# Attention and two MLPs on one core: due times of weight conversions and of transposed copies

## The chip, the cores and the metric

One core of a Trainium2 chip runs the whole program. The metric is the device time of one execution in microseconds; below 0.5% two kernels cannot be told apart.

## The reference

Attention over 2 batches and 12 heads of 448 positions and 64 dimensions, with scores capped by tanh, and then two MLPs of 768 to 2048 to 768 on the 896 tokens that come out:

```python
scores = cap * np.tanh(np.matmul(q, k.transpose(0, 1, 3, 2)) / np.sqrt(64) / cap)
attn = np.exp(scores - np.max(scores, axis=-1, keepdims=True))
attn = attn / (np.sum(attn, axis=-1, keepdims=True) + 1e-09)
x = np.matmul(attn, v)                      # then heads side by side: 896 x 768
h = x @ w_in;  g = np.where(h > 0, h, np.exp(np.minimum(h, 0)) - 1);  x = g @ w_out
h = x @ w_in2; out = np.maximum(0.01 * h, h) @ w_out2
```

The inputs are float32 but for the weights, which come as 64-bit floats (two 32-bit words each).

## The kernel before

**Attention.** Two heads of one batch make a pair; there are twelve, numbered 0 to 11. For a pair TensorE transposes k and q (L343, tiles `ntk`, `ntq`, which share one PSUM bank), VectorE copies them out (L358 `kT`; L354 `qT`, with a scale), TensorE makes the scores in four pieces (L371, `sc10.0` to `sc10.3` for pair 10; two banks of PSUM take turns), ScalarE takes tanh and exp (L391, L399, tiles `e10.0`, `e10.1` of two pieces each), POOL adds the two pieces of each (L408, `s10.0`, `s10.1`) and VectorE adds the halves (L414). TensorE multiplies with v (L496, `po`) and sums the rows (L510, `sm`); VectorE takes the reciprocal (L516, `rec`) and multiplies (L524, `xf`). ScalarE rounds that to the short format (L303, `xh`) and VectorE takes the remainder (L306, `xl`): each product of the MLPs is three products of rounded parts and remainders. The steps of neighbouring pairs are interleaved: the reciprocal of pair n falls between the scores of pairs n+1 and n+2, and the transposes for pair n+1 beside those of pair n.

**Weights.** `w_in` comes in slabs (`g1.0` to `g1.15` for the first MLP), `w_out` in slabs `o1.00.0` and so on. For each, SyncE loads the raw words (L549, `raw...`, three buffers), ScalarE scales the upper word (L555, `wg1.0`), VectorE shifts the lower word right (L562; for later slabs ScalarE does this, L567) and merges it and the sign in (L576, L585). `split` then rounds (ScalarE, L303, `g1.0h`) and takes the remainder (VectorE, L306, `g1.0l`). So one early slab of w_in costs VectorE four steps. The MLP's first product (L646) needs `g1.0h` and `g1.0l`.

**The order.** Nothing is in the order of the code. `plan(engine, cost, fn, ...)` records a step; `Plan.order()` runs all of them against a table of costs, engine by engine, and always takes the step that can start first and, among those, the one with the smallest `late` (the latest start that keeps its due time and those of its followers). The engines then execute their lists in that order, and a step that waits holds up all behind it on its engine. A step with `calm` (conversions due before `TM`, and `xh` and `xl`) may not be placed more than `AHEAD` before its `late` (L125). POOL's adds, `xl`, the adds of halves and the VectorE steps of conversions are marked `port`: the planner never lets two of them overlap. `TP = 9.0` is the planner's time for a pair, `TM = 12.6 * TP` its end of attention; the three first slabs are due 24 us before it and later (L878).

Of the kernel before, what the change touches and what calls it, by code (L numbers as in the profile page):

```python
# [23 lines left out]
class Plan:  # L24
# [8 lines left out]

    LATENCY = dict(PE=0.27, ACT=0.12, DVE=0.1, POOL=0.1, SP=0.1)
    LANDING = 2.0
    AHEAD = 12.0
    STAY = 2.0
    SWITCH = 0.12

# [33 lines left out]
    def order(self):  # L73
# [39 lines left out]
        def earliest(o):  # L113
# [10 lines left out]
            if o["calm"]:  # L124
                t = max(t, o["late"] - self.AHEAD)  # L125
            if o["gp"]:
# [67 lines left out]
def attention_elu_mlp_leaky_mlp(  # L194
# [55 lines left out]
    with tc.If((bits & 0x7FFFFFFF) <= CAP_BOUND_BITS, preferred_fallthrough_block=True) as small:  # L250
        block(*args, bounded=True)
    with small.Else():
        block(*args, bounded=False)
# [3 lines left out]
def block(ctx, tc, consts, q, k, v, w_in1, w_out1, w_in2, w_out2, out, bounded):  # L257
# [37 lines left out]
    plan = Plan(CAPACITY)  # L295
    V = {}

    def tl(pool, tag, name, shape, dtype=F32):
        V[name] = pools[pool].tile(shape, dtype, tag=tag, name=name, bufs=CAPACITY[tag])
        return V[name]  # L300
# [33 lines left out]
    def transpose_nat(nm, n, at):  # L334

        name, pt = f"{nm}T{n}", f"nt{nm}{n}"

        tag = "sm" if n == 0 and nm == "q" else "nt"

        def fn():  # L340
            t = tl("ps", tag, pt, [P, 512])
            for c in range(NC):
                nc.tensor.matmul(  # L343
                    t[:, c * CP : (c + 1) * CP], V[f"n{nm}{n}"][:, c], ident[:CP, :CP],
                    is_transpose=True, start=True, stop=True,
                )

        plan("PE", 0.39, fn, reads=[f"n{nm}{n}"], writes=[pt], new={pt: tag}, at=at, att=True,
             kind="transpose")

        def evacuate():
            t = tl("att", nm + "T", name, [P, S])
            if nm == "q":
                nc.vector.tensor_scalar(  # L354
                    out=t, in0=V[pt][:, :S], scalar1=qscale, scalar2=None, op0=ALU.mult
                )
            else:
                nc.vector.tensor_copy(t, V[pt][:, :S])  # L358

        plan("DVE", 0.6, evacuate, reads=[pt], writes=[name], new={name: nm + "T"}, att=True)  # L360

    def scores(n, c, at):

# [228 lines left out]
    def split(name, to, due=None):  # L592
        hi, lo = to + "h", to + "l"
        calm = CALM if due is not None and due < TM else 0.0
        plan("ACT", 0.73, lambda: rounded(tl("w", "whi", hi, V[name].shape, F32R), V[name]),
             reads=[name], writes=[hi], new={hi: "whi"}, due=due, calm=calm)
        plan("DVE", 0.87, lambda: remainder(tl("w", "wlo", lo, V[name].shape, F32R), V[hi], V[name]),
             reads=[name, hi], writes=[lo], new={lo: "wlo"}, port=True, due=due, calm=calm)

    def in_src(w, m):  # L600
        return w[:, m * P : (m + 1) * P, :].rearrange("(k p) f t -> p k f t", p=P)

    def out_src(w, k2, half):
        src = w[2 * k2 * P : (2 * k2 + 2) * P, half * HALF : (half + 1) * HALF, :]
        return src.rearrange("(k p) e t -> p k e t", p=P)
# [243 lines left out]
    for n in range(NPAIR):  # L849
        T = (n + 0.3) * TP  # L850
        load("k", k, n)
        load("q", q, n)
        load("v", v, n)
        transpose_nat("k", n, T - 0.95 * TP)
        transpose_nat("q", n, T - 0.8 * TP)
        if n == 0:

            plan("PE", 0.4, lambda: nc.tensor.matmul(
                tl("ps", "po", "unused", [P, 512])[:, :P], busy, busy, start=True, stop=True),
                writes=["unused"], new={"unused": "po"}, at=T - 0.7 * TP, att=True)  # L860
        for c in range(NC):
            scores(n, c, T + c * TP / 4)
        (bounded_softmax if bounded else row_softmax)(n)
        for c in range(NC):
            attend(n, c, T + (c + 3.6) * TP / 4)
        if bounded:
            sums(n, T + 7.4 * TP / 4)
        x1(n, T + 2.6 * TP)
    TH = 6 * KM * MM
    TO = 3 * MS * (KF // 2) * MM  # L870
    T0 = TM
    for nm, w_in, w_out in (("1", w_in1, w_out1), ("2", w_in2, w_out2)):
        slabs = [(i, h, k2) for i, h in ((0, 0), (1, 0), (1, 1), (0, 1)) for k2 in range(K2)]
        for m in range(KF):
            due = T0 + m * TH - 12.0
            if nm == "1" and m < 3:

                due = min(due, T0 - 24.0 + 2.5 * m)  # L878
            convert(f"g{nm}.{m}", in_src(w_in, m), f"wg{nm}.{m}", "wa", due)
            split(f"wg{nm}.{m}", f"g{nm}.{m}", due + 2.0)  # L880
            hidden(nm, m, T0 + m * TH)
        for x, (i, h, k2) in enumerate(slabs):
            due = T0 + (x + 1) * TH if nm == "2" else TM + x * KF * TH / len(slabs)
            convert(f"o{nm}.{i}{h}.{k2}", out_src(w_out, h * K2 + k2, i), f"w{nm}.{i}{h}.{k2}", "w", due)
        products(nm, T0 + KF * TH)
        T0 += KF * TH + 7 * TO
# [44 lines left out]
```

## Time and profile before

| | us |
|---|---|
| median of 3 runs | 575.94 (574.22 to 576.28) |
| profiled execution, own time | 572.52 |
| its span | 570.7 |
| TensorE busy | 554.6 (97%) |
| VectorE busy | 482.8 (85%) |
| ScalarE busy | 386.6 (68%) |
| POOL busy | 53.9 (9%) |
| mean granted TensorE clock | 0.994 |
| loads of k, q, v: issue to landing, median | 3.3, 3.4, 2.7 |

Busy time is the union of an engine's instructions; the granted clock is a share of full speed. Times in the rows are counted from the start of the span. The attention takes the first 115 us, the first MLP runs to about 335 us, the second to the end.

### The profile page before, as it was taken

The page shows a single profiled execution, that of the slowest core. Times are in us where ns is not written, and L with a number is a line of the kernel's source. Part 1 is how long each engine was busy: PE and PEld are TensorE (multiplying, and loading weights), DVE is VectorE, ACT ScalarE, POOL GpSimd, SP SyncE. Part 2 cuts the span into 40 slices and gives each one's busy share as a digit, 9 for nine tenths or more (in the row PEclk, how much of TensorE's full clock was granted, in tenths as well). Part 3 has the DMA queues.
Part 4 walks back from the last instruction along what each step waited for, and adds up shares of the span by engine and source line. Part 5 has one row for each costly group of instructions (what it writes and reads, how often), then busy time and mean ns, then how long its engine had stood idle before and what let it go on. Part 6 is the DMA issues. An engine that isn't in the chain of part 4 may idle for free.

```text
span 570.7 us, 7409 instructions
## 1 busy us (share of the span) xinstructions
PE 554.6 (97%) x2750; PEld 452.7 (79%) x2750; DVE 482.8 (85%) x628; ACT 386.6 (68%) x539; POOL 53.9 (9%) x32
## 2 busy tenths in 40 slices
PE   8999998899999999999999999999999999999995
PEld 4333333279999999899989999999999999889994
DVE  2698899896888998999999978888997599997662
ACT  5888997946888888865566766766775255645550
POOL 2544544410000000000000000000000000000000
PEclk9999998999999999999999999999999999999998
DMA  8933324215767777500012117766672000001112
GB/s 157 249 68 96 82 65 128 71 57 172 224 206 203 198 215 219 168 2 1 1 55 56 56 57 222 208 199 206 208 202 83 0 2 1 1 1 48 49 35 68
DMA packets 61435, 61.89 MB, mean 108 GB/s; under 512 B 23248, under 2 KB 53200, under 8 KB 61392
## 3 DMA queue, kind: packets, MB, share of 16 engines
q1 hardware_dynamic: 61120, 61.23, 38.2%
q8 instruction: 23, 0.38, 0.3%
q14 instruction: 20, 0.16, 0.1%
q10 hardware_dynamic: 240, 0.11, 0.1%
q0 software_dynamic: 32, 0.00, 0.0%
HBM read 58.59 MB, written 2.75 MB: 107 GB/s over the span
## 4 chain that ended last, share of the span: by engine, by line
PE 80%; DVE 10%; ACT 6%; issue 2%; POOL 1%; DMA 1%; SPq 0%; DVEq 0%; ACTq 0%; POOLq 0%
PE acc L646 27%; PE acc L751 23%; PE acs L751 11%; PE po L496 2%; DVE rec L516 2%; PE sm L510 1%; PE ct L807 1%; DMA firstq<-in_q_dram 1%; PE acs29.1_3302 L646 1%; PE acs6.0_1238 L646 1%; PE acs35.0_3687 L646 1%; PE acs32.0_3491 L646 1%; PE acs26.1_3112 L646 1%; PE acs12.1_1635 L646 1%; PE acs3.1_1022 L646 1%
## 5 line engine op out<-in xcount | busy, mean ns | idle before, releaser
L516 DVE RECIPROCAL rec<-sm 128x448 f32<-128x448 f32 x12 | 35.4, 2954 | 3.1 <-PE sm L510 3.0
L358 DVE COPY kT<-ntk 128x448 f32<-128x448 f32 x12 | 7.5, 622 | 7.4 <-PE ntk L343 7.0
L822 ACT COPY ob<-ct 112x512 f32<-112x512 f32 (+1 forms) x8 | 4.5, 560 | 10.5 <-PE ct L807 10.2
L343 PEld LDWEIGHTS ntq<-ident,nq 112*128 112x128 f32 x44 | 4.3, 140 | 8.8 <-DVE kT L358 8.1
L354 DVE TENSOR_SCALAR qT<-ntq,qscale 128x448 f32<-128x448 f32 x12 | 8.2, 681 | 3.5 <-PE ntq L343 3.5
L343 PEld LDWEIGHTS ntk<-ident,nk 112*128 112x128 f32 x44 | 4.3, 140 | 7.8 <-issue 7.1
L524 DVE TENSOR_TENSOR xf<-po,rec 128x448 f32<-128x448 f32 x12 | 7.5, 625 | 0.4
L343 PE MATMUL ntq<-ident,nq 112*128 112x112 f32 x44 | 6.6, 273 | 0.8 <-DVE kT L358 0.8
L343 PE MATMUL ntk<-ident,nk 112*128 112x112 f32 x44 | 6.6, 273 | 0.0
L567 ACT ACTIVATE rawo1.00.2_978<-rawo1.00.2_978,third 128x768 int32<-128x768 uint8 x1 | 1.0, 1028 | 7.8 <-DMA rawo1.00.2_978<-in_moe_w_out_dram 7.8
L371 PE MATMUL sc10.0_795<-qT,kT 64*112 64x448 f32 x4 | 1.8, 1010 | 2.6 <-DVE qT L354 2.6
L675 ACT ACTIVATE ea2.14.0_3955<-acs38.0_3883 128x448 f32<-128x448 f32 x1 | 0.5, 546 | 5.4 <-PE acs38.0_3883 L646 5.4
L820 DVE COPY ob<-ct 112x512 f32<-112x512 f32 (+1 forms) x5 | 3.2, 637 | 1.1 <-ACT ob L822 0.6
L666 DVE SCALAR_TENSOR_TENSOR gg1.0.0_1080<-ea1.0.0_1068,acc 128x448 f32<-128x448 f32 x1 | 0.6, 620 | 4.1 <-ACT ea1.0.0_1068 L663 4.1
L660 ACT ACTIVATE ea1.0.0_1068<-acc 128x448 f32<-128x448 f32 x1 | 0.5, 547 | 5.1 <-DMA rawo1.00.3_1049<-in_moe_w_out_dram 5.1
L238 PE MATMUL unused<-busy 128*128 128x128 f32 x12 | 2.9, 434 | 1.1 <-DVE third L244 1.1
L303 ACT CAST th2.7.3_4004<-gg2.3.1_3278 128x448 fp32r<-128x448 f32 x1 | 0.6, 569 | 5.0 <-PE acs L751 5.0
L391 ACT ACTIVATE e0.0_155<-sc0.0_147 112x896 f32<-112x896 f32 x1 | 0.9, 917 | 4.0 <-PE sc0.0_147 L371 4.0
L238 PEld LDWEIGHTS unused<-busy 128*128 128x128 f32 x12 | 2.6, 330 | 1.1 <-DVE third L244 1.1
L788 DVE TENSOR_TENSOR c2.00.0_4963<-u2.1.0_4292,acc 128x448 f32<-128x448 f32 x1 | 0.6, 621 | 3.2 <-PE acc L751 3.2
L263 DVE TENSOR_SCALAR ncap<-capb 128x1 f32<-128x1 f32 x1 | 0.2, 154 | 3.7 <-DMA capb<-in_cap_dram 3.7
L408 POOL TENSOR_TENSOR s9.0_787<-e9.0_733 112x896 f32<-112x896 f32 x1 | 3.0, 3050 | 2.2 <-ACT e9.0_733 L399 2.2
(4974 smaller groups left out, 2266.9 us busy)
## 6 DMA issues: line engine op xcount, KB each, us to landing
nv<-in_v_dram SPq DMA_DIRECT2D x12, 224.0 KB, 2.7
nk<-in_k_dram SPq DMA_DIRECT2D x11, 224.0 KB, 3.3
nq<-in_q_dram SPq DMA_DIRECT2D x11, 224.0 KB, 3.4
out_dram<-ob SPq DMA_DIRECT2D x3, 672.0 KB, 4.3
rawg1.0_203<-in_moe_w_in_dram SPq DMA_DIRECT2D x1, 768.0 KB, 7.3
rawg1.1_248<-in_moe_w_in_dram SPq DMA_DIRECT2D x1, 768.0 KB, 6.1
rawg1.2_282<-in_moe_w_in_dram SPq DMA_DIRECT2D x1, 768.0 KB, 7.5
rawo1.00.0_764<-in_moe_w_out_dram SPq DMA_DIRECT2D x1, 768.0 KB, 4.9
```

The lines of the kernel that those rows point to most:

```text
L238: nc.tensor.matmul(t, busy, busy, start=True, stop=True)
L343: nc.tensor.matmul(t[:, c * CP : (c + 1) * CP], V[f"n{nm}{n}"][:, c], ident[:CP, :CP], is_transpose=True, start=True, stop=True,)
L354: nc.vector.tensor_scalar(out=t, in0=V[pt][:, :S], scalar1=qscale, scalar2=None, op0=ALU.mult)
L358: nc.vector.tensor_copy(t, V[pt][:, :S])
L496: nc.tensor.matmul(V[po][j * D : (j + 1) * D, :S], V[f"nv{n}"][:, j, c], V[e][:, c % 2, j], start=(c == 0), stop=(c == NC - 1),)
L510: nc.tensor.matmul(t[j * D : (j + 1) * D, :S], ones[:CP], V[f"s{n}.0"][:, j], start=True, stop=True,)
L516: plan("DVE", 2.97, lambda: nc.vector.reciprocal(out=tl("att", "rec", rec, [P, S]), in_=V[sm][:, :S]), reads=[sm], writes=[rec], new={rec: ...
L524: nc.vector.tensor_tensor(out=tl("att", "xf", xf, [P, S]), in0=V[po][:, :S], in1=V[f"rec{n}"], op=ALU.mult)
L646: nc.tensor.matmul(bank(where[b]), V[g + w][:, kt, :], V[f"{part}{nm}.{b}.{kt}"], start=(x == 0 and i == 0), stop=(x == KM - 1 and i == 2),)
L751: nc.tensor.matmul(bank(where[m]), V[sp][:, kt % 2, m * P : (m + 1) * P], V[tp], start=(kt == 0 and i == 0), stop=(kt == KF // 2 - 1 and i ...
L807: nc.tensor.matmul(t[:CP, x * P : (x + 1) * P], V[c][:, x * CP : (x + 1) * CP], ident, is_transpose=True, start=True, stop=True,)
L822: nc.scalar.copy(dst, src)
```

## The change

Three numbers. The planner may place a calm step 60 us ahead of its latest start instead of 12. The copies `kT` and `qT` get a due time 2 us behind the planned time of their transposes (before, they inherited theirs from the scores that read them). The first three slabs of w_in are due 18 us before the end of attention instead of 24.

```diff
     LANDING = 2.0
-    AHEAD = 12.0
+    AHEAD = 60.0
     STAY = 2.0
@@ transpose_nat
-        plan("DVE", 0.6, evacuate, reads=[pt], writes=[name], new={name: nm + "T"}, att=True)
+        plan("DVE", 0.6, evacuate, reads=[pt], writes=[name], new={name: nm + "T"}, att=True, due=at + 2.0)
@@ the loop over slabs
             if nm == "1" and m < 3:
-                due = min(due, T0 - 24.0 + 2.5 * m)
+                due = min(due, T0 - 18.0 + 2.5 * m)
```

What that does to the lists is seen at three places. On VectorE (DVE), between the copy of k and the copy of q for pair 10, the list of before reads:

```order
L358 COPY kT_745<-ntk_737 128x448
L576 SCALAR_TENSOR_TENSOR wg1.0_700<-wg1.0_700,rawg1.0_203 128x768
L585 SCALAR_TENSOR_TENSOR wg1.0_700<-rawg1.0_203,wg1.0_700 128x768
L414 TENSOR_TENSOR s8.0_696<-s8.0_696,s8.1_728 112x896
L562 TENSOR_SCALAR rawg1.1_248<-rawg1.1_248 128x768
L576 SCALAR_TENSOR_TENSOR wg1.1_726<-wg1.1_726,rawg1.1_248 128x768
L306 TENSOR_TENSOR xl1.1.3_781<-xf_735,xh1.1.3_761 128x448
L585 SCALAR_TENSOR_TENSOR wg1.1_726<-rawg1.1_248,wg1.1_726 128x768
L354 TENSOR_SCALAR qT_789<-ntq_749,qscale 128x448
L516 RECIPROCAL rec_793<-sm_773 128x448
```

and now, at the same copies:

```order
L358 COPY kT_765<-ntk_757 128x448
L414 TENSOR_TENSOR s8.0_716<-s8.0_716,s8.1_748 112x896
L354 TENSOR_SCALAR qT_777<-ntq_769,qscale 128x448
L562 TENSOR_SCALAR rawg1.2_282<-rawg1.2_282 128x768
L306 TENSOR_TENSOR xl1.1.3_801<-xf_755,xh1.1.3_779 128x448
L516 RECIPROCAL rec_803<-sm_792 128x448
L524 TENSOR_TENSOR xf_825<-po_735,rec_803 128x448
L414 TENSOR_TENSOR s9.0_787<-s9.0_787,s9.1_808 112x896
L358 COPY kT_834<-ntk_820 128x448
```

The conversions of slabs 0 and 1 have left this place. They stand some four pairs earlier. There, on VectorE, from the reciprocal of pair 4 to that of pair 5, the list of before has none:

```order
L516 RECIPROCAL rec_521<-sm_510 128x448
L524 TENSOR_TENSOR xf_535<-po_452,rec_521 128x448
L414 TENSOR_TENSOR s5.0_503<-s5.0_503,s5.1_525 112x896
L358 COPY kT_549<-ntk_537 128x448
L354 TENSOR_SCALAR qT_563<-ntq_553,qscale 128x448
L306 TENSOR_TENSOR xl1.0.2_580<-xf_535,xh1.0.2_565 128x448
L516 RECIPROCAL rec_586<-sm_576 128x448
```

and now:

```order
L585 SCALAR_TENSOR_TENSOR wg1.0_396<-rawg1.0_203,wg1.0_396 128x768
L516 RECIPROCAL rec_526<-sm_519 128x448
L524 TENSOR_TENSOR xf_544<-po_458,rec_526 128x448
L306 TENSOR_TENSOR xl1.1.1_552<-xf_476,xh1.1.1_504 128x448
L358 COPY kT_558<-ntk_546 128x448
L414 TENSOR_TENSOR s5.0_512<-s5.0_512,s5.1_532 112x896
L562 TENSOR_SCALAR rawg1.1_248<-rawg1.1_248 128x768
L354 TENSOR_SCALAR qT_577<-ntq_564,qscale 128x448
L306 TENSOR_TENSOR xl1.0.2_593<-xf_544,xh1.0.2_575 128x448
L576 SCALAR_TENSOR_TENSOR wg1.1_403<-wg1.1_403,rawg1.1_248 128x768
L516 RECIPROCAL rec_602<-sm_589 128x448
```

A merge of slab 0, a shift and a merge of slab 1 have come in, the copy `kT` stands ahead of the add of halves, and the `xl` of the pair before has moved behind the reciprocal. On TensorE (PE) the list changes little up to pair 10; from the third piece of its scores to the sums of pair 10 it reads before:

```order
L343 MATMUL ntq_826<-ident,nq_702 128x112 x4
L371 MATMUL sc10.2_833<-qT_789,kT_745 112x448 x2
L371 MATMUL sc10.3_841<-qT_789,kT_745 112x448 x2
L496 MATMUL po_849<-e10.0_807,nv_791 64x448 x2
L510 MATMUL sm_857<-s9.0_787,ones 64x448 x2
L496 MATMUL po_849<-e10.0_807,nv_791 64x448 x2
L371 MATMUL sc11.0_865<-qT_855,kT_822 112x448 x2
L371 MATMUL sc11.1_869<-qT_855,kT_822 112x448 x2
L496 MATMUL po_849<-e10.1_847,nv_791 64x448 x4
```

and now:

```order
L371 MATMUL sc10.2_836<-qT_777,kT_765 112x448 x2
L343 MATMUL ntq_846<-ident,nq_720 128x112 x4
L371 MATMUL sc10.3_853<-qT_777,kT_765 112x448 x2
L371 MATMUL sc11.0_860<-qT_858,kT_834 112x448 x2
L510 MATMUL sm_865<-s9.0_787,ones 64x448 x2
L496 MATMUL po_870<-e10.0_818,nv_795 64x448 x4
L496 MATMUL po_870<-e10.1_851,nv_795 64x448 x2
L371 MATMUL sc11.1_886<-qT_858,kT_834 112x448 x2
```

The first scores of pair 11 have moved up to the last of pair 10, and the sums and `po` behind them. Besides, both halves of `po` of `e6.1` now stand ahead of `ntq` in pair 7. ScalarE's list takes up `wg1.0` and `wg1.1` (L555) in front of `e4.0`, `g1.0h` in front of `e6.0`, steps of `o1.00.0` around `e6.1`, `wg1.2` in front of `e7.1`, `g1.1h` behind `e8.1` and two steps of `o1.00.1` behind `e9.1`. On SyncE the load of `rawo1.00.0` stands ahead of the load of v for pair 6, some ten loads earlier than before. POOL's list is the same.

## Rows read from the trace of the kernel before

**Rows 1.** TensorE's waits: line, releaser, us in total, times, longest.
```profile
PE sc10.0_795 L371 <- DVE qT L354: 2.6, 1, 2.6
PE sm L510 <- DVE s10.0_853 L414: 1.6, 1, 1.6
...
PE sm L510 <- DVE s9.0_787 L414: 1.0, 1, 1.0
PE ntq L343 <- DVE kT L358: 0.8, 4, 0.3
```
**Rows 2.** Windows: pairs 4 to 7, then pair 8 to the MLP (columns: Rows 3).
```profile
39.00:73.50 34.50, 34.17 (x178) 13.25 (x176) 31.46 (x25) 30.46 (x29) 16.71 (x8) 1.00 0.33 81
73.50:113.85 40.35, 34.94 (x170) 12.79 (x168) 37.95 (x32) 35.77 (x36) 18.95 (x8) 0.96 0.32 87
```
**Rows 3.** Windows: us, busy PE, PEld, DVE, ACT, POOL, clock, DMA: pairs 9, 10.
```profile
82.27:83.96 1.69, 1.69 (x11) 0.63 (x9) 1.66 (x2) 1.69 (x3) 0.81 (x1) 1.00 0.00 0
...
93.48:96.54 3.06, 3.06 (x8) 1.13 (x8) 3.02 (x2) 1.04 (x2) 1.21 (x1) 0.54 0.81 216
```
**Rows 4.** Timeline of VectorE ahead of pair 10: start us, us, instruction, idle before.
```profile
85.14 0.95 DVE L576 SCALAR_TENSOR_TENSOR wg1.0_700<-wg1.0_700,rawg1.0_203 128x768 int32<-128x768 int32 x1
...
88.00 0.56 DVE L562 TENSOR_SCALAR rawg1.1_248<-rawg1.1_248 128x768 int32<-128x768 int32 x1
88.67 2.67 DVE L576 SCALAR_TENSOR_TENSOR wg1.1_726<-wg1.1_726,rawg1.1_248 128x768 int32<-128x768 int32 x1
91.25 0.62 DVE L306 TENSOR_TENSOR xl1.1.3_781<-xf,xh1.1.3_761 128x448 fp32r<-128x448 f32 x1
...
92.66 0.68 DVE L354 TENSOR_SCALAR qT<-ntq,qscale 128x448 f32<-128x448 f32 x1
```
**Rows 5.** Timeline of VectorE in pairs 4 to 6.
```profile
44.37 2.05 DVE L306 TENSOR_TENSOR xl1.0.1_450<-xf,xh1.0.1_435 128x448 fp32r<-128x448 f32 x1
...
50.09 0.62 DVE L358 COPY kT<-ntk 128x448 f32<-128x448 f32 x1
...
55.09 2.94 DVE L516 RECIPROCAL rec<-sm 128x448 f32<-128x448 f32 x1
```
**Rows 6.** Timeline of POOL: two of its adds.
```profile
43.86 2.09 POOL L408 TENSOR_TENSOR s4.0_437<-e4.0_403 112x896 f32<-112x896 f32 x1 [2.44 <-ACT e4.0_403 L399]
...
87.47 3.05 POOL L408 TENSOR_TENSOR s9.0_787<-e9.0_733 112x896 f32<-112x896 f32 x1 [2.22 <-ACT e9.0_733 L399]
```
**Rows 7.** Timeline of ScalarE: a wait in pair 4, a conversion in pair 8.
```profile
40.14 0.92 ACT L391 ACTIVATE e4.0_403<-sc4.0_397 112x896 f32<-112x896 f32 x1 [0.88 <-PE sc4.0_397 L371]
...
78.64 0.91 ACT L555 ACTIVATE wg1.0_700<-rawg1.0_203 128x768 f32<-128x768 f32 x1
```
**Rows 8.** Timeline of TensorE: `ntq` in pairs 5, 9; `po` in 6, 7.
```profile
50.89 0.60 PE L343 MATMUL ntq<-ident,nq 112*128 112x112 f32 x4
...
63.41 1.67 PE L496 MATMUL po<-e6.0_533,nv 112*64 112x448 f32 x8
...
70.37 0.97 PE L496 MATMUL po<-e6.1_574,nv 112*64 112x448 f32 x4
...
85.40 0.60 PE L343 MATMUL ntq<-ident,nq 112*128 112x112 f32 x4
```
**Rows 9.** Timeline of VectorE and TensorE: adds of halves, first product of the MLP.
```profile
99.93 2.98 DVE L414 TENSOR_TENSOR s9.0_787<-s9.0_787,s9.1_805 112x896 f32<-112x896 f32 x1
...
109.92 2.98 DVE L414 TENSOR_TENSOR s10.0_853<-s10.0_853,s10.1_872 112x896 f32<-112x896 f32 x1
...
113.85 0.47 PE L646 MATMUL acc<-xh1.0.0_301,g1.0h 128*128 128x448 f32 x1
```
**Rows 10.** Timeline of the first MLP: ScalarE behind `g1.0`, remainder and load of `g1.3`.
```profile
134.31 0.55 ACT L660 ACTIVATE ea1.0.0_1068<-acc 128x448 f32<-128x448 f32 x1 [5.11 <-DMA rawo1.00.3_1049<-in_moe_w_out_dram]
...
136.97 0.96 DVE L306 TENSOR_TENSOR g1.3l<-wg1.3_963,g1.3h 128x768 fp32r<-128x768 f32 x1
...
139.46 0.19 PEld L646 LDWEIGHTS acc<-xh1.0.0_301,g1.3l 128*128 128x128 f32 x1
```

## The prediction

> **What bounds the kernel now.** The page's first part gives TensorE 554.6 us of a 570.7 us span, so I looked only for the places where TensorE does not run, and asked the view of its waits first [rows 1]. Three waits carry nearly all of it, and all three are waits for VectorE in the last third of the attention: 2.6 us before the scores of pair 10 (for `qT`, the scaled transpose of q), and 1.0 and 1.6 us before the row sums `sm` of pairs 9 and 10 (for the add of `s9.0` and `s10.0`). The windows say the same by stage [rows 2]: in pairs 4 to 7 (39.0 to 73.5) TensorE is busy 34.17 of 34.5 us, from pair 8 to the first product of the MLP (73.5 to 113.85) 34.94 of 40.35. VectorE is nearly full in both, 31.46 of 34.5 and 37.95 of 40.35.
>
> The first wait costs more than itself. The granted clock is 1.00 while TensorE runs on, and 0.54 in the 3.06 us behind the 2.64 us gap [rows 3], which is about the lower of its two levels (1.2 against 2.4 GHz): two scores and their hand-over take 3.06 us there, the same pieces of pair 9 take 1.69. That is 1.37 us more. After the gaps of 1.04 and 1.57 us no such stretch follows.
>
> Why `qT` is late is seen in VectorE's queue [rows 4]. Between the copy of k and that of q stand five steps of the w_in conversions, and one of them (L576 at 88.67) takes 2.67 us where its twin at 85.14 takes 0.95. POOL's add ran from 87.47 to 90.52 then [rows 6], and the step ended 0.8 us behind it. `xl` shows the same at 44.37 (2.05 us, POOL's add at 43.86) against 0.62 at 91.25 [rows 4 to 6]. So a VectorE step that meets POOL's add waits for its end: 1.43 us more in `xl`, 1.72 in a merge. The adds of `s9.0` and `s10.0` took 2.98 us for that reason [rows 9].
>
> **The change, part by part.** No work is added or removed; the whole effect is in the order. The planner may now begin a conversion 60 us ahead of its due time instead of 12, and the copies of transposes have a due time, so that they go ahead of conversions.
>
> *What leaves.* The order shows that in place of the seven steps between the copies of k and q of pair 10 (an add, `xl` and five of conversions) one add is left, and `qT` follows at once; before the adds of pairs 9 and 10 no conversion stands any more. So the three waits go, 2.64 + 1.04 + 1.57 = 5.25, and with the long gap the slow stretch, 1.37. Ceiling: 6.6 us. What was 6.6 us late is then next bound by TensorE itself at the pitch of pairs 4 to 7 [rows 2].
>
> *What arrives on VectorE.* Three slabs of four steps, 0.56 + 3 x 0.95 = 3.4 us each [rows 4], 10.2 us over pairs 4 to 10: 1.46 us a pair. Four pairs show 34.5 - 31.46 = 3.04 us idle, 0.76 a pair [rows 2]. That alone would be too little. But of a pair's busy time 1.43 us is `xl` waiting for POOL: when VectorE comes to `xl` later, `xl` still ends when POOL's add ends, and the delay is swallowed. The room is 0.76 + 1.43 = 2.2 us against 1.46. This is the cover that my forecast rests on; it fails where POOL's add is itself pushed later.
>
> *New waits.* TensorE feels VectorE through `kT`: `ntq` follows `kT` within 0.2 us [rows 5, 8], so a reciprocal that starts late shows at `ntq` at once.
> (a) Pairs 4 and 5: ScalarE gets two conversions of 0.9 us [rows 7] into a wait of 0.88. tanh, POOL's add and `xl` slide by 0.9, the reciprocal by 0.75, and 0.15 is cover: `ntq` at 50.89 waits 0.6. Bounds 0 and 0.9.
> (b) Pair 6: the copy of k now goes ahead of the add; its old wait of some 0.16 goes.
> (c) Pairs 6 and 7: the shift (0.56) and a merge (0.95) put the reciprocal 1.5 late [rows 4]. TensorE is 0.45 late by then, and the half of `po` that stood at 70.37 (0.97) and now goes ahead of `ntq` covers 0.85 [rows 8]: 0.2. By this walk the shift and POOL's add come within some 0.2 us of each other; if the shift loses, 1.1.
> (d) Pairs 8 and 9: a merge (0.95) holds POOL's add back, the add holds `xl`, and ScalarE is late by one conversion (0.9): the reciprocal starts 1.8 late, TensorE is 0.6 late and 0.15 is cover: `ntq` at 85.40 waits 1.0. Bounds 0 and 1.9.
> (e) Pairs 10 and 11: pair 11's first scores now stand right behind those of pair 10, where half a `po`, the sums and the other half stood between. They need the bank that tanh frees and `qT`: I take 0.55, between 0 and 1.0.
> Together 0.6 + 0.2 + 1.0 + 0.55 = 2.35; of the 0.8 us of old waits for `kT` [rows 1] three, 0.5 us, go. Net 1.85. None of these waits is longer than the 1.57 us behind which the clock stayed up, so no slow stretch is added.
>
> *Queues.* On SyncE the load of `rawo1.00.0` moves ten loads forward and waits there for the last merge of slab 0; that merge stands just before the reciprocal of 55.09 [rows 5], and the first load behind it is v of pair 6, which TensorE uses at 63.41 [rows 8]: 8 us, against 2.7 us for such a load to land (the page's part on DMA issues), so no cost. ScalarE receives three steps of about 0.9 us more within the attention (two w_out slabs); where it has no room is counted in (a) and (d).
>
> *Is the gain kept?* Behind the attention TensorE is full; the slab nearest to its use is `g1.3`: its remainder ends at 137.93, TensorE loads it at 139.46, 1.5 us of slack [rows 10]. Its chain hangs on the end of TensorE's own group for `g1.0` (`ea1.0.0` at 134.31), so it slides with TensorE, and the gain stays.
>
> *Sum.* 6.6 - 1.85 = 4.8 us (6.62 unrounded, to 4.77): the first product, at 113.85 now [rows 9], comes at about 109.1, and the profiled execution goes from 572.52 (570.7 of span and 1.8 around it) to 567.7. That execution lies 3.4 under the median of the runs, 575.94; I take the difference off the median: 571.1.
>
> *A rule against it.* The rows show that the one who starts first makes the other wait: L576 2.67 behind POOL, and POOL's add 3.05 behind two VectorE steps [rows 4, 6]. The Trainium skill says this as a rule (SBUF — State Buffer, "Who interferes with whom"): a VectorE instruction with two inputs in SBUF and a GpSimd instruction that reads SBUF cannot share the port, and whoever comes first blocks the other for the whole instruction. The trace agrees (2.67 against 0.95). If by that rule every moved two-input step met an add, it would be the second rival below.
>
> **The rivals.**
> *The races go wrong, the gain is eaten.* Nine merges and remainders and three shifts move to where POOL's add runs about half the time (16.71 of 34.5 us [rows 2]). If two more than I counted lose, at 1.43 to 1.72 us, and reach TensorE in full, 2.9 to 3.4 us of the 4.8 are gone: 574.0 to 574.5. For it: VectorE's room is thin. Against: `xl` waits for POOL once a pair and resets the lateness. 20%.
> *VectorE becomes the bound (slower).* Price: 1.46 us a pair of work, and one lost race of 1.72 a pair, less the 0.76 idle, if `xl` swallows nothing: 2.4 us x 7 pairs = 17 us, less 6.6: 586. It decides when the extra per pair passes 0.76 + 6.6/7 = 1.7 us; the work alone is 1.46, so a single lost race in seven pairs would do if the cover in `xl` were not there. Against: the 2.05 us of `xl` [rows 5] show the cover. 8%.
> *The gain is given back in the MLP.* The profile names a load (`rawo1.00.3`) as what released `ea1.0.0` [rows 10]. If that is true and the load does not move, `g1.3` comes no sooner and TensorE keeps only the 1.5 us of slack: 574.4. Against: `ea1.0.0` reads the bank of `g1.0`, so it cannot start ahead of TensorE's last product for it, whatever the load does. 4%.
> The order itself shows that the change does what it says.
>
> **How the numbers follow.** Forecast 68%: gains between 3 and 6.6 us, 569.3 to 573. The gained 6.6 and the 0.5 of old waits give the lowest end, 568.9; the first and third rival reach 574.5. With the spread of the runs (574.22 to 576.28) the range 569.0 to 575.0 leaves out the slower rival and a few per cent on each side. About 0.5%, 2.9 us, is what a measurement of this kernel can tell from no change. Faster by more: 70% (the forecast and the better end of the first rival). Within: 22%. Slower: 8%, the second rival.
>
> **What would show it.** In the profile after: no wait for `qT` at pair 10, granted clock 1.00 from 90 to 100 us; the adds of `s9.0` and `s10.0` at about 1.1 us; the first product of the MLP near 109; waits of `ntq` for `kT` of 0.5 to 1 us in pairs 5 and 9, more than 0.8 in total; `g1.3`'s remainder still ahead of its load. Wrong if TensorE's waits for `kT` sum to over 4 us, if VectorE is busy at 97% from pair 4 on with merges of 2 us and more, or if TensorE waits for `g1.3` to `g1.5`.

## The result

The changed kernel takes 567.83 us (median, 567.63 to 570.78) where the kernel before takes 575.16 us (574.22 to 576.28) beside it. The medians lie 7.3 us apart; the ratio of the runs (it is not the quotient of the medians) is 0.9895, 95% interval 0.9867 to 0.9924, or 6.0 us less. A second comparison, made beside the last experiments, gave 568.74 against 573.91, ratio 0.9925 (0.9898 to 0.9951). The forecast, 571.1 against a median of 575.94 or a ratio of 0.9916, lies between the two ratios, and faster was its likeliest case. Its range, 569.0 to 575.0, holds the time by the ratio (0.9895 of 575.94 is 569.9); the median itself lies 1.2 us below it.

TensorE's waits in the changed kernel (waiting instruction, its line, what released it, us in total, times, longest), where [rows 1] stood:

```profile
PE ntq L343 <- DVE kT L358: 1.4, 3, 0.7
...
PE acc L751 <- DVE tl1.3.3_2611 L306: 1.1, 1, 1.1
```

The waits for `qT` of pair 10 and for the adds of `s9.0` and `s10.0` are gone. What is left in the attention is 1.4 us for `kT`. The second row is in the first MLP; that wait was 0.2 us before.

The windows of the changed kernel, to be held against [rows 2] and [rows 3] (us, busy PE, PEld, DVE, ACT, POOL with instructions, granted clock, DMA share, GB/s):

```profile
39.00:73.50 34.50, 34.09 (x178) 13.25 (x176) 34.36 (x31) 33.45 (x33) 16.24 (x8) 1.00 0.46 109
73.50:109.20 35.70, 34.90 (x176) 12.57 (x172) 34.50 (x29) 34.45 (x35) 17.86 (x9) 1.00 0.28 78
93.00:96.00 3.00, 3.00 (x18) 1.25 (x18) 2.97 (x4) 2.97 (x5) 1.82 (x1) 1.00 0.01 2
```

In the second stretch TensorE stood still 5.41 us in 40.35 before, and 0.80 in 35.70 now. The clock stays at 1.00 where it had fallen to 0.54. VectorE, 31.46 of 34.5 us busy in pairs 4 to 7 before, is now busy 34.36 of 34.5.

VectorE in pair 5 and around pair 10, the counterpart of [rows 4, 9] (start us, us, instruction, idle before it):

```profile
53.97 2.69 DVE L585 SCALAR_TENSOR_TENSOR wg1.0_396<-rawg1.0_203,wg1.0_396 128x768 int32<-128x768 int32 x1
...
88.22 0.68 DVE L354 TENSOR_SCALAR qT<-ntq,qscale 128x448 f32<-128x448 f32 x1
88.82 2.19 DVE L562 TENSOR_SCALAR rawg1.2_282<-rawg1.2_282 128x768 int32<-128x768 int32 x1
...
94.98 1.08 DVE L414 TENSOR_TENSOR s9.0_787<-s9.0_787,s9.1_808 112x896 f32<-112x896 f32 x1
...
105.07 1.08 DVE L414 TENSOR_TENSOR s10.0_856<-s10.0_856,s10.1_882 112x896 f32<-112x896 f32 x1
```

Conversion steps still meet POOL's adds (2.69 at 53.97, 2.19 at 88.82). But `qT` of pair 10 is now done ahead of the one that loses 1.6 us, and both adds take 1.08 us where they took 2.98. On TensorE (same columns; [rows 8, 9] before):

```profile
52.51 0.60 PE L343 MATMUL ntq<-ident,nq 112*128 112x112 f32 x4 [0.41 <-DVE kT L358]
...
70.30 0.60 PE L343 MATMUL ntq<-ident,nq 112*128 112x112 f32 x4
...
87.36 0.60 PE L343 MATMUL ntq<-ident,nq 112*128 112x112 f32 x4 [0.72 <-DVE kT L358]
...
98.09 1.01 PE L371 MATMUL sc10.3_853<-qT,kT 64*112 64x448 f32 x4
99.17 1.01 PE L371 MATMUL sc11.0_860<-qT,kT 64*112 64x448 f32 x4
...
109.21 0.47 PE L646 MATMUL acc<-xh1.0.0_301,g1.0h 128*128 128x448 f32 x1
```

The first product of the MLP moved from 113.85 to 109.21. The two profiles do not begin alike: the first scores of pair 4 stand at 39.02 before and at 40.39 after. In that execution TensorE's very first scores took 1.83 us (at 7.14), in the profile of before 1.01 (at 6.73); the same kernel in e12 has 1.01 again, and its scores of pair 4 stand at 38.93. So the late start belongs to the execution and not to the change, and I compare by stage, from those scores to the first product: 74.83 us before, 68.82 after, **6.01 less**. From the first product to the end it is 456.9 (570.7 - 113.85) and 456.6. The forecast had the first product at 109.1 and the profiled execution at 567.7; they came at 109.21 and 567.63. That both fit so closely is luck: the late start took back 1.37 us of a gain that was larger than forecast.

Times of one kernel spread over 2 to 7 us in these comparisons. A row from the middle of the second MLP, of the changed kernel and then of the same kernel in e12, shows why (window, us, busy PE with its count, clock, DMA share, GB/s):

```profile
400.00:430.00 30.00, 30.00 (x150) 1.00 0.70 208
```

```profile
400.00:430.00 30.00, 30.00 (x147) 1.00 0.70 206
```

The same products, with TensorE never idle and the clock granted in full, run at 150 or at 147 in 30 us, for long stretches that change from one execution to the next. Over 450 us of MLP that is up to 9 us (an estimate: 2% of it) which no change to the attention explains. For the experiments I therefore give, beside the time, the **stage** in the profile from the first scores of pair 4 to a product that has 2144 others behind it in every kernel (15.9 us behind the first product of the MLP in the kernel before): all of the attention lies ahead of it, whichever way its last pieces are ordered. A stage is from one execution each; the changed kernel's came out alike in two (84.63 and 84.62). Each ratio is against runs of the kernel before beside it (medians 573.99 for e1 to e4, 574.41 for e5 to e8, 573.91 for e9 to e12), not against the first row.

| kernel | median us | ratio to before (95%) | stage us |
|---|---|---|---|
| before | 575.16 | | 90.70 |
| changed | 567.83 | 0.9895 (0.9867 to 0.9924) | 84.63 |
| e1 copies' due time alone | 573.42 | 0.9985 (0.9961 to 1.0009) | 90.15 |
| e2 60 us alone | 570.71 | 0.9916 (0.9884 to 0.9948) | 87.25 |
| e3 60 us and copies | 567.18 | 0.9878 (0.9841 to 0.9915) | 83.98 |
| e4 copies and slabs | 574.13 | 0.9989 (0.9965 to 1.0012) | 88.43 |
| e5 before, gap filled | 572.77 | 0.9972 (0.9949 to 0.9994) | 90.11 |
| e6 changed, qT twice | 568.59 | 0.9900 (0.9872 to 0.9928) | 85.33 |
| e7 changed, xl twice | 570.95 | 0.9935 (0.9906 to 0.9963) | 87.74 |
| e8 24 us in place of 60 | 576.75 | 1.0026 (0.9997 to 1.0055) | 91.68 |
| e9 changed, 9 steps left out | 566.68 | 0.9878 (0.9853 to 0.9904) | 84.39 |
| e10 90 us in place of 60 | 565.58 | 0.9865 (0.9845 to 0.9885) | 84.06 |
| e11 90 us, slabs due as before | 567.61 | 0.9898 (0.9868 to 0.9929) | 84.17 |
| e12 changed, again | 568.74 | 0.9925 (0.9898 to 0.9951) | 84.62 |

### The profile page after: what moved, and what is told of

Read it like the earlier page. It is cut to its first block, busy times and chain, and to the rows that moved or that the text cites. A ratio compares the mean times of both kernels' runs of the same rounds, so it can differ in the third digit from the quotient of the medians.

```text
span 565.8 us, 7405 instructions
## 1 busy us (share of the span) xinstructions
PE 553.5 (98%) x2750; PEld 453.4 (80%) x2750; DVE 479.9 (85%) x628; ACT 385.6 (68%) x539; POOL 52.5 (9%) x32
## 4 chain that ended last, share of the span: by engine, by line
PE 86%; DVE 6%; ACT 4%; POOL 1%; issue 1%; DMA 1%; DVEq 0%; ACTq 0%; POOLq 0%
PE acc L646 28%; PE acc L751 24%; PE acs L751 12%; PE po L496 3%; DVE rec L516 2%; PE sm L510 1%; PE ct L807 1%; PE ntq L343 1%; DMA firstk<-in_k_dram 1%; PE acs35.0_3687 L646 1%; PE acs9.1_1437 L646 1%; PE acs29.1_3302 L646 1%; PE acs15.0_1845 L646 1%; PE acs26.1_3112 L646 1%; PE acs12.0_1632 L646 1%
```

## The experiments

Theory: what counts is that the conversions are spread over many pairs, where `xl`'s wait for POOL's add swallows them. Rivals: the copies' due time does it alone; VectorE is simply full; VectorE had room anyway. In kernels with added lines the line numbers in the rows are a few higher.

### Which of the three numbers carries the gain (e1 to e4, e8)

**e1**, the copies' due time alone:

```diff
-        plan("DVE", 0.6, evacuate, reads=[pt], writes=[name], new={name: nm + "T"}, att=True)
+        plan("DVE", 0.6, evacuate, reads=[pt], writes=[name], new={name: nm + "T"}, att=True, due=at + 2.0)
```

> Only the due time of the copies (conversions as before). In the order one merge is left between the copies of k and q of pair 10 (seven steps before), but eight conversion steps still stand between that copy of k and the add of s10.0. Theory 'spreading': the qT wait of 2.64 us and the slow stretch of 1.37 go, the waits of the row sums of pairs 9 and 10 stay (1.04 and 1.57, or up to 1 more): 4.0 us of the ceiling at the best, a time about 571 to 572. Rival 'the copies carry it': as fast as the whole change, about 568.

Measured: no difference (0.9985), the stage 0.55 us shorter. Both expectations missed. The wait for `qT` went, and another took its place. TensorE, then VectorE, then the window behind the wait, in e1:

```profile
100.83 0.60 PE L343 MATMUL ntq<-ident,nq 112*128 112x112 f32 x4 [3.06 <-DVE kT L358]
```

```profile
90.99 2.67 DVE L576 SCALAR_TENSOR_TENSOR wg1.1_726<-wg1.1_726,rawg1.1_248 128x768 int32<-128x768 int32 x1
93.58 2.51 DVE L306 TENSOR_TENSOR xl1.1.3_782<-xf,xh1.1.3_763 128x448 fp32r<-128x448 f32 x1
96.02 0.95 DVE L585 SCALAR_TENSOR_TENSOR wg1.1_726<-rawg1.1_248,wg1.1_726 128x768 int32<-128x768 int32 x1
96.88 0.56 DVE L562 TENSOR_SCALAR rawg1.2_282<-rawg1.2_282 128x768 int32<-128x768 int32 x1
97.35 2.94 DVE L516 RECIPROCAL rec<-sm 128x448 f32<-128x448 f32 x1
100.22 0.55 DVE L358 COPY kT<-ntk 128x448 f32<-128x448 f32 x1
```

```profile
102.50:106.00 3.50, 3.50 (x10) 0.94 (x8) 3.47 (x5) 2.40 (x4) 0.22 (x1) 0.51 0.00 0
```

The conversions that no longer stand between the copies of k and q stand ahead of the next reciprocal, and the next copy of k waits behind it: 3.06 us in place of 2.64, with the low clock (0.51) behind it as before. With the conversions in a heap it did not matter here which copy went ahead of which.

**e2**, the 60 us alone (`AHEAD = 12.0` to `60.0`, nothing else):

> Only the 60 us (no due time of copies, slabs due as before). All conversions of the first three slabs but one remainder stand ahead of the copy of k of pair 10, but between that copy and the one of q stand a reciprocal (about 3 us) and xl. Theory 'spreading': the adds of s9.0 and s10.0 come early and the row sums do not wait, at most 1.5 us of wait for qT of pair 10 is left and no slow stretch: 569 to 571. Rival 'the copies carry it': the wait for qT stays over 2 us with its slow stretch, 573 or more.

Measured 570.71, the stage 3.45 us shorter: within what spreading expects. No slow stretch, and no wait of the row sums; what is left in the attention are three waits of about a microsecond, only one of them for `qT`:

```profile
PE sc6.0_545 L371 <- ACT e5.1_511 L399: 1.2, 1, 1.2
PE sc10.0_823 L371 <- DVE qT L354: 1.1, 1, 1.1
PE sc9.0_738 L371 <- ACT e8.1_727 L391: 1.1, 1, 1.1
```

**e3**, the 60 us and the copies, slabs due as before:

> The whole change without the later due time of the slabs. Theory 'spreading': the slab's due time is of no weight, 567.5 to 569. Rival 'all three are needed': four conversion steps stand in front of the reciprocal of pair 8 and hold the transposes of pair 10 back by over 2 us: 570 or more.

Measured 567.18, stage 83.98: the whole change without its third number is as fast as with it.

**e4**, the due times of copies and slabs, without the 60 us:

> The due times of copies and slabs without the 60 us: the twelve conversion steps stand together in pairs 8 to 10. Theory 'spreading': no wait for qT of pair 10 over 1 us, but the adds of s9.0 and s10.0 are late as before, 2.5 us and more of waits for the row sums: 571 to 573. Rival 'the copies carry it': about 568.

Measured 574.13, ratio 0.9989: no gain that can be told, where I expected 1 to 3 us. I had expected the row sums to wait and they did not; the profile has 2.4 us of waits for `kT` and 1.9 and 0.8 for ScalarE instead, no low clock, and a stage 2.3 us shorter. Not every run is like it: seven of the twelve have a mean granted clock of 0.997 or 0.998 (median 572.8 us), five 0.994 to 0.996 (median 574.5), where none of the 26 runs of the kernel before beside them is above 0.996. So e4 may gain a little; the times do not show it.

**e8**, half way (`AHEAD = 24.0`, the rest as changed):

> The changed kernel with 24 us in place of 60: the twelve conversion steps stand in pairs 7 to 11 (in pairs 4 to 11 with 60, in 7 to 10 with 12), and between reciprocals there are up to four of them. Theory 'spreading is what counts': about half of the gain, 570 to 572 (waits of 2 to 4 us for kT, qT and the row sums). Rival 'it is enough that conversions begin a little earlier': as with 60, 567 to 569.

Measured 576.75, ratio 1.0026, the stage 0.98 us longer than before: both expectations missed. TensorE and VectorE in e8:

```profile
97.99 1.01 PE L343 MATMUL ntq<-ident,nq 112*128 112x112 f32 x4 [3.66 <-DVE kT L358]
```

```profile
87.21 2.71 DVE L585 SCALAR_TENSOR_TENSOR wg1.0_656<-rawg1.0_203,wg1.0_656 128x768 int32<-128x768 int32 x1
89.83 0.62 DVE L562 TENSOR_SCALAR rawg1.1_248<-rawg1.1_248 128x768 int32<-128x768 int32 x1
90.48 0.98 DVE L576 SCALAR_TENSOR_TENSOR wg1.1_663<-wg1.1_663,rawg1.1_248 128x768 int32<-128x768 int32 x1
91.36 2.52 DVE L306 TENSOR_TENSOR xl1.1.3_779<-xf,xh1.1.3_760 128x448 fp32r<-128x448 f32 x1
93.80 2.94 DVE L516 RECIPROCAL rec<-sm 128x448 f32<-128x448 f32 x1
```

Three conversion steps in a row ahead of `xl` are too many here: the first meets one POOL add (2.71), `xl` the next one (2.52), and the reciprocal comes late by all of it. The gain is not in proportion to the spreading. Nor does the number of steps in a pair decide it alone. The changed kernel has three between the reciprocals of pairs 8 and 9, and e3, with the shortest stage of all, has four between those of pairs 7 and 8, three of them behind `xl`. In e3:

```profile
89.09 1.93 DVE L306 TENSOR_TENSOR xl1.1.3_798<-xf,xh1.1.3_782 128x448 fp32r<-128x448 f32 x1
...
93.55 2.94 DVE L516 RECIPROCAL rec<-sm 128x448 f32<-128x448 f32 x1
96.42 0.55 DVE L358 COPY kT<-ntk 128x448 f32<-128x448 f32 x1
```

```profile
97.03 0.60 PE L343 MATMUL ntq<-ident,nq 112*128 112x112 f32 x4 [0.18 <-DVE kT L358]
```

Only `xl` met an add there, `kT` stands directly behind the reciprocal (in e8 behind `xf`), and TensorE's list has more work ahead of `ntq`: it loses 0.18 us, against 3.66.

### What the low clock was worth (e5)

```diff
+FILL = 7
...
             t = tl("ps", "sc", name, [P, 2, 512])
+            for _ in range(FILL if (n, c) == (10, 0) else 0):
+                nc.tensor.matmul(t[:, 0, :P], busy, busy, start=True, stop=True)
             for j in range(2):
```

> The kernel before, with seven products of a 128x128 tile put on TensorE into the free bank of sc10.0, ahead of those scores: TensorE has work in the 2.64 us in which it waited for qT, and nothing else is changed. Theory 'the gap brings the low clock': granted clock 1.00 from 90 to 100, the first scores of pair 10 at their usual 0.8 us spacing, and the stage from the scores of pair 4 to the first product 1.0 to 1.4 us shorter than before (74.83 there), the waits for the row sums as before. Rival 'the low clock comes by itself or costs nothing on the path': the 0.54 stays, or the stage stays within 0.4 us.

TensorE in e5, and two windows, over the old slow stretch and over a new one:

```profile
95.04 1.01 PE L374 MATMUL sc10.0_795<-qT,kT 64*112 64x448 f32 x4 [0.78 <-DVE qT L355]
95.89 0.92 PE L374 MATMUL sc10.1_809<-qT,kT 64*112 64x448 f32 x4
...
104.20 0.97 PE L513 MATMUL sm<-s9.0_787,ones 112*64 112x448 f32 x4 [1.91 <-DVE s9.0_787 L417]
```

```profile
105.40:108.90 3.50, 3.50 (x12) 1.08 (x8) 3.46 (x3) 1.12 (x2) 1.64 (x1) 0.51 0.00 0
93.00:96.00 3.00, 2.22 (x18) 1.64 (x18) 3.00 (x4) 1.43 (x2) 2.32 (x1) 1.00 0.56 82
```

With TensorE at work through the gap the clock stays at 1.00 and the scores of pair 10 come 0.85 us apart: the gap brought the low clock, as I had read it. But the stage gained 0.53 us to the first product (74.30 against 74.83), not 1.0 to 1.4. TensorE came to the row sums of pair 9 sooner and waited there for the same add, 1.91 us in place of 1.04, and this time the clock fell behind that wait; the wait for the add of `s10.0` (1.57 before) is gone in turn. So the low clock was moved and not taken away. The row sums of pair 9 start 63.56 us behind the first scores of pair 4, where it was 63.95: VectorE's lateness set the end of that stretch, and time won on TensorE alone was mostly handed back.

### Whether `xl` swallows what is put ahead of it (e6, e7, e9)

**e6** does the copy of `qT` twice in seven pairs, **e7** does `xl` twice in seven pairs; the order of everything else is that of the changed kernel.

```diff
             if nm == "q":
-                nc.vector.tensor_scalar(
+                for _ in range(2 if 5 <= n <= 11 else 1):
+                    nc.vector.tensor_scalar(
...
```

```diff
+        def low_half():
+            t = tl("x", "x", xl, [P, S], F32R)
+            for _ in range(2 if 2 <= n <= 8 else 1):
+                remainder(t, V[xh], V[src][:, :S])
```

> The changed kernel with the copy of qT done twice in pairs 5 to 11: 7 times 0.6 us more on VectorE, each directly ahead of xl or of a conversion step that waits for POOL's add. Theory 'xl swallows': xl and those steps end as before (about 2.0 us shrinks to 1.4), the stage from the scores of pair 4 to the first product grows by under 0.7 us (68.82 in the changed kernel). Rival 'VectorE is full and nothing swallows': plus 2.5 to 4.2 us. Rival 'VectorE has room anyway': under 0.7 here and in the next run too.

> The changed kernel with xl done twice for seven pairs: 7 times 0.55 us more on VectorE, each directly behind the step that waits for POOL's add and mostly ahead of the reciprocal. Theory 'xl swallows': here nothing swallows it, the reciprocals slide by 0.55 a pair, the waits of ntq for kT grow from 1.4 to over 3 us and the stage (68.82) by 2 to 3.9 us. Rival 'VectorE has room anyway': under 0.7. Rival 'nothing swallows': the same as in the run with qT twice.

The same `xl` in the changed kernel, in e6 (behind the double copy), and in e7 (twice):

```profile
46.23 2.17 DVE L306 TENSOR_TENSOR xl1.0.1_456<-xf,xh1.0.1_439 128x448 fp32r<-128x448 f32 x1
```

```profile
45.87 1.40 DVE L355 TENSOR_SCALAR qT<-ntq,qscale 128x448 f32<-128x448 f32 x2
47.18 1.47 DVE L306 TENSOR_TENSOR xl1.0.1_457<-xf,xh1.0.1_439 128x448 fp32r<-128x448 f32 x1
```

```profile
44.79 2.83 DVE L306 TENSOR_TENSOR xl1.0.1_456<-xf,xh1.0.1_439 128x448 fp32r<-128x448 f32 x2
```

With 0.7 us more ahead of it, `xl` takes 0.7 us less: it ends when POOL's add ends. With the step doubled behind that point VectorE loses 0.66 us. The stage says the same: e6 plus 0.70 us for 7 x 0.7 us of added work, with one new wait, 0.7 us of `sc11.0` for `qT`; the seven `xl` from the first scores of pair 4 to the first product shrink from 11.2 to 7.7 us in all. e7 is plus 3.11 us for 7 x 0.66 us, with the waits for `kT` at 3.9 us in place of 1.4. So for steps beside `xl` it matters whether they stand ahead of the wait for POOL or behind it. Both rivals fall.

**e9** leaves the shift, the merge and the sign of the three slabs out of the changed kernel:

```diff
+        bare = key in ("g1.0", "g1.1", "g1.2")
...
         def low():
...
+            if bare:
+                return
...
         def merge():
+            if bare:
+                return
...
         def sign():
+            if bare:
+                return
```

> The changed kernel with the shift, the merge and the sign of the first three w_in slabs left out (9 of the 12 conversion steps, 7.35 us of VectorE's work); the hidden layer is then computed from wrong weights. Theory 'xl swallows': what the moved steps still cost is what TensorE waits for kT and qT, about 1.5 us in all, so the stage from the scores of pair 4 to the first product goes from 68.8 to 67.2 to 68.2, no more, and xl waits longer for POOL. Rival 'VectorE's stretch is the bound': 3 us and more.

The stage is 0.24 us shorter, and the waits for `kT` still sum to 1.0 us. In e9, the window of pairs 4 to 7, and the reciprocal that stands at 56.59 in the changed kernel:

```profile
39.00:73.50 34.50, 34.09 (x180) 13.23 (x178) 30.03 (x26) 33.45 (x33) 16.13 (x8) 1.00 0.42 108
```

```profile
56.61 2.96 DVE L516 RECIPROCAL rec<-sm 128x448 f32<-128x448 f32 x1 [2.46 <-PE sm L510]
```

7.35 us of VectorE's work are gone, VectorE is 4.3 us less busy in this window, and TensorE is busy for the same 34.09 us. The reciprocal starts at the same time; where L585 stood, VectorE now waits 2.46 us for the row sums. So a VectorE that is busy 99.6% of a stretch was not its bound. What stays of the waits for `kT` is not due to these nine steps; the conversions on ScalarE and the three remainders are still in place in e9.

Two things limit what e9 says. From the first scores of pair 4 to the first product TensorE is busy 67.61 of 68.82 us in the changed kernel, so 1.2 us of TensorE's waiting was the most that could be gained there. And the moved steps did not live on `xl`'s wait in the main. The changed kernel over that stage, then e9:

```profile
40.39:109.21 68.82, 67.61 (x346) 25.53 (x345) 67.49 (x57) 66.52 (x67) 34.11 (x16) 1.00 0.36 92
```

```profile
40.50:109.07 68.57, 67.60 (x347) 25.55 (x345) 60.57 (x49) 66.30 (x67) 33.38 (x16) 1.00 0.35 92
```

```profile
DVE rec L516 <- PE sm L510: 4.3, 3, 2.5
```

Without the steps VectorE is idle 8.0 us where it was 1.3, and 4.3 of them are waits of the reciprocal for the row sums (the last row, of e9; 0.8 in the changed kernel). The seven `xl` take 13.3 us in place of 11.2, but two of the moved steps themselves lost 1.74 and 1.64 us to POOL's adds. So what took the moved steps was mostly time in which VectorE has nothing to do while TensorE works; `xl`'s wait can swallow work too, as e6 shows, but took little of these steps.

### Further out (e10, e11), and the changed kernel again (e12)

> The changed kernel with 90 us in place of 60: the conversions begin in pair 2 and there is never more than two steps between a copy of k and its reciprocal ahead. Theory 'spreading counts': as fast as with 60 or up to 1 us faster (566.5 to 568), waits for kT under 1.4. Rival 'too early is dear too' (the loads of the first pairs and POOL's adds meet them): 569 or more.

> 90 us, copies with their due time, the slabs due as before the change (24 in place of 18): the conversions reach from pair 2 to pair 9. Theory 'spreading counts': 566 to 568, the best of all if the waits for kT fall under 0.5. Rival 'too early is dear too': 569 or more.

> The changed kernel itself beside the other three: 567 to 568.5, the stage from the scores of pair 4 to the first product 68.5 to 69.2.

With 90 us the conversions reach into pair 2. The waits of `ntq` in e10 (e11 has the same row):

```profile
PE ntq L343 <- DVE kT L358: 0.9, 2, 0.7
```

The stages, 84.06 and 84.17, are some 0.5 us shorter than that of the changed kernel (84.62 beside them), and e3's is as short (83.98). By the times e10 is the best of all, 565.58 against 568.74, but behind the stage, where both do the same work, its profile shows 440.6 us and that of e12 443.7, so the times can't carry a difference of this size. A gain of half a microsecond over the change is what the profiles carry; from 60 us on nothing much is left to win here.

## Why the prediction was right, point by point

**What leaves.** Right: the three waits and the slow stretch are all gone, and both adds took 1.08 us (forecast about 1.1). But the 6.6 us were not four separate terms. e5 shows that they hang together: with the gap filled the low clock and the wait came back further on, and 0.53 of the 1.37 us was gained. The sum holds, as I read it, because the change took VectorE's lateness itself.

**What arrives on VectorE.** The cover that the forecast rested on was there and thicker than I had it: I left 2.2 - 1.46 us a pair as room, e9 shows that 7.35 us of the moved work cost 0.24. That `xl`'s wait is such cover is right (e6 against e7), but it is not the cover that the moved steps used in the main: in e9 VectorE has 8.0 us of idle time over seven pairs, where I had counted 0.76 a pair, 5.3, and the steps took 6.7 of it. That part of the mechanism was right only in its result. One of my own signs of failure was badly chosen, too: VectorE is busy 68.86 of 70.20 us (98%) from pair 4 to the first product and a step of 0.95 us did take over 2 (2.69 at 53.97), yet next to nothing was lost: in e9, without that step, VectorE waits at the same place for the row sums.

**New waits.** This is the term that was mis-sized. (a) 0.41 against 0.6, (c) 0 against 0.2 (the shift won its race with POOL's add, as I had walked it), (d) 0.72 against 1.0, (e) 0.24 against 0.55 (the scores of pairs 10 and 11 stand 1.08 us apart where 0.84 is usual). Together 1.37 against 2.35. (a), (d) and (e) lie within their bounds, in the middle or below it; I took the middle or more. The old wait for `kT` that is left is 1.4 - 0.41 - 0.72 = 0.27, as forecast (0.3). That is 0.98 of the 1.24 us by which the stage gained more than forecast (6.01 against 4.77); the rest I cannot place. As to cause, (a) and (d) named ScalarE's conversions as well as VectorE's steps; with nine of the latter out (e9), 1.0 of the 1.4 us of `kT` waits stays, so the share of these nine is the smaller one.

**The port rule.** The Trainium skill (SBUF — State Buffer, "Who interferes with whom") has whoever comes first block the other; the rows agree, 2.69 us for a step with two inputs that takes 0.95 alone. The shift, with one input, lost as well (2.19 us in place of 0.55), which the rule as the prediction gives it, for two inputs, does not cover. The rule did not bring the second rival about: where the merge lost, at 53.97, e9 shows that the reciprocal behind it starts no sooner without it. In e1 and e8, with two losses close together (2.67 and 2.51, 2.71 and 2.52), it goes with the loss of the gain.

**Queues and the MLP.** No wait for a load was added behind the head. The third rival fell: in the changed kernel

```profile
131.05 0.96 DVE L306 TENSOR_TENSOR g1.3l<-wg1.3_950,g1.3h 128x768 fp32r<-128x768 f32 x1
...
133.53 0.19 PEld L646 LDWEIGHTS acc<-xh1.0.0_301,g1.3l 128*128 128x128 f32 x1
```

the remainder of `g1.3` ends 1.5 us ahead of its load, the slack of [rows 10] to a tenth. Not foreseen: the wait for `tl1.3.3` in the first MLP, 1.1 us in place of 0.2. It is 0.2 to 1.1 us in most of the kernels and gone in e2 and e11; what decides it I have not settled.

**What the forecast did not say.** It took the change as one piece. Two of its three numbers bring no gain that the times can tell without the first (e1, e4), the third brings nothing with the others (e3), and the first alone brings about half to four fifths: 3.45 of 6.07 us by the stage, 4.8 of 6.0 by the ratios. The first and third without the second were not run.

## What to carry to other kernels

An engine that shows as full need not be the bound: look for the step that waits for another engine's end in every round. Work put ahead of that step cost little here (0.7 of about 5 us in e6); behind it, it cost most of its length (3.1 of 4.6 us in e7). Spread low-urgency work over many rounds, and test whether it costs by leaving it out. Giving the urgent step a due time did not help while the low-urgency work stood in a heap, since the next urgent step then waited for the heap. A stall that several engines share is not the sum of its parts: filling the gap on the waiting engine alone gained 0.53 of 1.37 us.

## What the runs showed of the hardware

- TensorE runs the same products at two paces with the granted clock at 1.00 throughout: 150 or 147 in 30 us (about 203 and 207 ns each over 75 products in a row), for stretches of 60 to 400 us. They differ between executions of one and the same kernel (the changed kernel and e12). What sets the pace is open.
- The granted clock fell to 0.50 at gaps of 2.64 us (before), 3.06 (e1), 3.66 (e8) and 1.91 (e5), and did not at gaps of 1.57 (before) and 1.89 (e4). With the 3.66 us it was low for 6.8 us, with the others for 3.4. In the kernel before and in e8 it fell before the gap had ended, in e1 and e5 1.7 and 1.2 us behind it, and gaps of 1.9 us went both ways: the length of the gap does not decide alone.
- VectorE's one-input shift on a 128x768 integer tile is held up by POOL's add too: 2.19 us against 0.55 (add at 88.50 for 2.09, shift at 88.82, in the changed kernel).
